# When the softmax sums are added: some adds moved behind the reciprocals, and one of GpSimd's adds moved to VectorE

## The chip, the cores and the metric

The kernel runs on one core of a Trainium2 chip. Its five compute engines run side by side, each through its own list of instructions, and meet by semaphores: TensorE (PE; PEld is its weight load), VectorE (DVE), ScalarE (ACT), GpSimd (POOL) and SyncE (SP), which here only starts DMA transfers. The metric is the device time of one execution in microseconds (us). Lower is better.

## The reference

Attention with normalised queries and keys for 8 batches, 12 heads, 448 tokens and a head size of 64; then a "mixture of depths", in which a gate picks 128 of the 448 tokens of each batch and only those go through two layers.

```python
def rmsnorm(x, g):
    rms = np.sqrt(np.mean(x * x, axis=-1, keepdims=True) + 1e-06)
    return x / rms * g
q_n, k_n = (rmsnorm(q, g_q), rmsnorm(k, g_k))
scores = scale * np.matmul(q_n, k_n.transpose(0, 1, 3, 2))
scores = scores - np.max(scores, axis=-1, keepdims=True)
attn = np.exp(scores)
attn = attn / (np.sum(attn, axis=-1, keepdims=True) + 1e-09)
x = np.matmul(attn, v)                      # then (B, S, heads * 64)
# ...
scores = np.einsum('bsd,d->bs', x, w_gate)
out = x.copy()
for b in range(B):
    top_idx = np.argpartition(-scores[b], capacity)[:capacity]
    xe = x[b, top_idx]
    h = np.maximum(xe @ w1, 0.0)
    ye = h @ w2
    g = 1.0 / (1.0 + np.exp(-scores[b, top_idx]))
    out[b, top_idx] = x[b, top_idx] + g[:, None] * ye
```

The change is about one line of this, `np.sum(attn, axis=-1)`: the denominators of the softmax.

## The kernel before

Four heads of one batch are a group n (24 groups, three to a batch). A group's keys come in seven pieces of 64, and one piece is a unit, `u = 7 * n + i`. For each unit TensorE computes scores (16 matmuls for two units), ScalarE their exponentials `p`, and TensorE multiplies `p` with the values into `av`, which is summed over the seven units. The denominators take another path. The `p` of a group are added up elementwise, mostly on VectorE; then TensorE sums over the keys (`den_ps`), ScalarE copies the sums out, TensorE turns them (`denT_ps`), VectorE takes reciprocals (`rden`), and VectorE multiplies the turned values (`x_ps`) with them. That gives `x`.

Which engine adds what. In the first six groups GpSimd adds units 0 and 1 into a spare tile (named `tok` in the trace), VectorE adds units 2 to 5 and then GpSimd's tile to them, and unit 6 goes to TensorE as it is:

```python
def add_probs(u):
    n, i = divmod(u, NI)
    if i == NI - 1 and sums_last(n):
        lasts.setdefault(n, []).append(probs.pop(u))
        return
    first = 2 if by_pool(n) else 0
    if first and i == 1:
        t = first_tokens[n % 2].rearrange("p h i d -> p h (i d)")
        nc.gpsimd.tensor_tensor(out=t, in0=probs.pop(u - 1), in1=probs.pop(u), op=OP.add)    # L332
        firsts[n] = t
    elif i > first:
        begins = i == first + 1
        if begins:
            sums[n] = p_pool.tile([128, 2, S], F32, name="sum", bufs=2)
        nc.vector.tensor_tensor(                                                             # L338
            out=sums[n], in0=probs.pop(u - 1) if begins else sums[n], in1=probs.pop(u), op=OP.add
        )
        if first and i == NI - 2:
            nc.vector.tensor_tensor(out=sums[n], in0=sums[n], in1=firsts.pop(n), op=OP.add)  # L342

def sums_last(n):
    return n < 2 * NG or n == n_groups - 1       # NG = 3

def by_pool(n):
    return n < 2 * NG
```

The sums over the keys, the reciprocals, and `x`. In the early steps `denT_ps` and the second `x_ps` of a group lie in the same bank of PSUM (`ps_moe`, one buffer), and `den_ps` and the first `x_ps` in another (`ps_aux`, one buffer), with exceptions by the flag `spare`:

```python
def sum_keys(n):
    ps = aux([128, 512], "den_ps")
    terms = [sums.pop(n)] + lasts.pop(n, [])
    # ... 8 matmuls per term                     (L372)
    nc.scalar.copy(out=den.rearrange("d j p -> d (j p)"), in_=ps[:, 0 : S // 2])
    dens[n] = den
    if n < n_groups - 1:
        q, place = now
        when = (q, place + 1) if place == 0 or long_next(q) else (q + 1, 0)
        tasks.insert(0, (when, lambda: invert_sums(n)))

def invert_sums(n):
    den = dens.pop(n)
    # ... two transposes into denT_ps            (L397)
    nc.vector.reciprocal(out=rden, in_=ps[:CP]...)                                           # L399

def to_tokens(n, c):
    # ... four transposes into x_ps              (L415)
    nc.vector.tensor_tensor(out=xs[b]..., in0=ps[:CP]..., in1=rdens[n]..., op=OP.mult)       # L417
```

The order of the work. A step q computes the scores of four units in two halves and lets the values of earlier units follow. `opening(q, place)` runs at most one or two due tasks: a group's tasks are `sum_keys` in the step in which its last unit is done, `invert_sums` and `to_tokens(n, 0)` at the start of the next, and then `to_tokens(n, 1)` with the gate. `run(slots)` issues the preparation of later groups: squares, `ss`, powers (`rinv`), scaled queries (`qT`) and loads. Instructions stay in the order in which they are issued, engine by engine:

```python
def before_layers(q):
    return done == 0 and ready.get(0, q + 1) > q       # the first batch's layers haven't begun

def run_values(upto, q):
    ended = False
    while waiting and waiting[0] <= upto:
        u = waiting[0]
        if ended and u % NI == 0:
            return
        values(waiting.pop(0))
        if u % NI == NI - 1:
            values_out(u // NI)
            finish(u // NI, q)
            ended = True
        add_probs(u)

while done < B or tasks:
    now[:] = q, 0
    k = PER * q                                        # PER = 4
    for half in range(HALVES):                         # HALVES = 2
        for u in (k + 2 * half, k + 2 * half + 1):
            if u < units:
                scores(u)
        run_values(k + 2 * half - 1, q)
    opening(q, 0)
    for half in range(HALVES):
        slots = (k + 2 * half, k + 2 * half + 1)
        if not short(q):
            run(slots)
        some = piece(q)                                # a piece of the two layers
        spare[0] = not some and half == 0
        if some or half == 0 or len(tasks) > 2:
            opening(q, half + 1)
        spare[0] = False
        run(slots)
    q += 1
```

Of the kernel before, what the change touches and what calls it, by code (L numbers as in the profile page):

```python
# [68 lines left out]
def fast(  # L69
# [30 lines left out]
    NG = H // GH  # L100
# [183 lines left out]
    def scores(u):  # L284
        n, i = divmod(u, NI)
        scs = [ps_sc.tile([128, 512], F32, tag="sc", name="sc") for _ in range(2)]


        for c in range(2):
            for hh in (1, 0):  # L290
                r = slice(D * hh, D * (hh + 1))
                nc.tensor.matmul(  # L292
                    out=scs[hh][D * c : D * (c + 1), 0:S],
                    lhsT=get("kT", n)[r, c, D * i : D * (i + 1)],
                    rhs=get("qT", n)[r, c, :],
                    start=True,
                    stop=True,
                )
        p = p_pool.tile([128, 2, S], F32, name="p")
        for hh in range(2):  # L300
            nc.scalar.activation(  # L301
                out=p[:, hh],
                in_=scs[hh][:, 0:S],
                func=AF.Exp,
                scale=rinvs[n, 1][:, hh, i : i + 1],
            )
        probs[u] = p

    def values(u):
        n, i = divmod(u, NI)  # L310
        if i == 0:
            avs[n] = [ps_av.tile([128, 512], F32, name="av") for _ in range(2)]
        for hh in (1, 0):
            for c in range(2):
                r = slice(D * c, D * (c + 1))
                nc.tensor.matmul(  # L316
                    out=avs[n][c][D * hh : D * (hh + 1), 0:S],
                    lhsT=get("v", n)[r, hh, i, :],
                    rhs=probs[u][r, hh],
                    start=(i == 0),  # L320
                    stop=(i == NI - 1),
# [22 lines that stand above are left out]
    def values_out(n):  # L344
        for c in (1, 0):
            t = norm_pool.tile([128, NJ, CP], F32, name="xT", bufs=4)
            nc.scalar.copy(out=t.rearrange("d j p -> d (j p)"), in_=avs[n][c][:, 0:S])
            xTs[n, c] = t
        avs.pop(n)

    dens, lasts, firsts = {}, {}, {}
# [3 lines left out]
    def sums_last(n):  # L355


        return n < 2 * NG or n == n_groups - 1

    def by_pool(n):  # L360

        return n < 2 * NG

    def sum_keys(n):

# [270 lines left out]
    HALVES = 2  # L636
# [12 lines left out]
    def opening(q, place):  # L649
        now[:] = q, place  # L650
        for _ in range(2):
            for i, (when, fn) in enumerate(tasks[:2]):
                if when <= (q, place):
                    tasks.pop(i)
                    waited = len(dens)
                    fn()
                    if place == 0 and len(dens) < waited:

                        break
                    return  # L660
                if i == 0 and dens:

                    return
# [27 lines left out]
    def finish(n, q):  # L691

        if n == n_groups - 1:
            for fn, args in ((sum_keys, (n,)), (invert_sums, (n,)), (to_tokens, (n, 0))):
                task((q, 1), fn, *args)
            task((q, 1), last_tokens, n)
            return
        task((q, 1), sum_keys, n)
        task((q + 1, 0), to_tokens, n, 0)
        task((q + 1, 1), last_tokens, n)  # L700
# [7 lines left out]
    def before_layers(q):  # L708
        return done == 0 and ready.get(0, q + 1) > q
# [33 lines left out]

        return -(-(units + 2 * PER - NG * NI * (B - 2 - b)) // PER)

    def run_values(upto, q):
        ended = False
        while waiting and waiting[0] <= upto:
            u = waiting[0]
# [5 lines that stand above are left out]
                values_out(u // NI)  # L755
                finish(u // NI, q)
                ended = True
            add_probs(u)

    for i in range(2):  # L760
        sum_squares(0, i, squares(0, i))
# [6 lines left out]
    def run(slots):  # L768
        for slot in sorted(x for x in todo if x < 0 or x in slots):
            for fn in todo.pop(slot):  # L770
                fn()

    def short(q):

        return pieces[0] == 1

    def piece(q):

        nonlocal moe, done
        if q in begin and pieces[0] > 2 and half == 1:  # L780
            return False
        pieces[0] += 1
        if next(moe, moe) is not moe:
            return True
        if ready.get(done, q + 1) > q:
            return False
        moe = mixture(done)
        done += 1
        pieces[0] = 1
        next(moe)  # L790
        return True
# [5 lines left out]
    moe, ready, done, q = iter(()), {}, 0, 0  # L797
    while done < B or tasks:
        now[:] = q, 0
        k = PER * q  # L800
        for half in range(HALVES):
            for u in (k + 2 * half, k + 2 * half + 1):
                if u < units:
                    scores(u)
            run_values(k + 2 * half - 1, q)
        opening(q, 0)
        for half in range(HALVES):
            slots = (k + 2 * half, k + 2 * half + 1)
            if not short(q):
                run(slots)  # L810
            some = piece(q)
# [6 lines that stand above are left out]
# [457 lines left out]
def _build(nc, ap, cap, out):  # L1275
    D = ap["g_q"].shape[0]
    with tile.TileContext(nc) as tc, ExitStack() as ctx:
        load_pool = ctx.enter_context(tc.tile_pool(name="load", bufs=1))
        with tc.tile_pool(name="bound", bufs=1) as pool:
            g = pool.tile([1, 2, D], F32, name="g")  # L1280
            nc.sync.dma_start(out=g, in_=ap["g_row"])
            loads = Loads(nc, load_pool, *(ap[n] for n in ("qT", "kT", "vp", "tok", "g2")))


            prod = pool.tile([1, D], F32, name="prod")
            nc.vector.tensor_mul(out=prod, in0=g[:, 0], in1=g[:, 1])
            nc.vector.tensor_mul(out=prod, in0=prod, in1=prod)
            top = pool.tile([1, 1], F32, name="top")
            nc.vector.tensor_reduce(out=top, in_=prod, axis=AX.X, op=OP.max)
            small = pool.tile([1, 1], I32, name="small")  # L1290
            nc.vector.tensor_scalar(
                out=small,
                in0=top,
                scalar1=MAX_SCORE * MAX_SCORE / D,
                scalar2=None,
                op0=OP.is_le,
            )
            is_small = nc.values_load(small[0:1, 0:1], min_val=0, max_val=1,
                skip_runtime_bounds_check_because="a comparison gives 0 or 1")
        with tc.If(is_small > 0) as cmp, tc.manual_schedule():  # L1300
            fast(
                tc, loads, *(ap[n] for n in _INS[5:]), cap, out,
            )
        with cmp.Else():
            general(tc, *(ap[n] for n in _INS), cap, out)
# [45 lines left out]
```

## Time and profile before

| | |
|---|---|
| time, median of 3 runs | 525.54 us (523.82 to 526.93) |
| span of the profiled run | 523.3 us |
| busy of TensorE, VectorE, ScalarE, GpSimd | 504.8, 339.9, 277.6, 195.7 us |
| mean granted clock of TensorE | 0.995 |
| GpSimd's adds (L332) | 6, mean 2240 ns |
| VectorE's adds (L338, the most common form) | 101, mean 1090 ns |
| VectorE's adds of GpSimd's tile (L342) | 6, mean 1408 ns |

The profile is one execution. A line of a timeline gives the start and the length in us, the engine, the line of the kernel, the operation, what it writes and reads, and in brackets how long its engine had stood idle and what ended that. A line of the waits gives who waited for whom, the total in us, how often, and the longest. A line of the window table gives the stretch, its length, and for PE, PEld, DVE, ACT and POOL the busy us and instructions; then the clock granted to TensorE as a share of full speed, the share of the DMA engines and GB/s. The line numbers are those of the whole kernel; the comments above repeat the ones that matter.

### The profile page before, as it was taken

Reading aid. Unit: us, or ns where it says so; the run is one execution under the profiler, and the core shown is the slowest. Engines: PE = TensorE matmul, PEld = TensorE weight load, DVE = VectorE, ACT = ScalarE, POOL = GpSimd, SP = SyncE. Lnnn points to the kernel's source line nnn. Section 1 sums busy time; section 2 is a strip of 40 time slices with the busy share of each in tenths; the row PEclk is TensorE's granted clock in tenths of the full one; section 3 lists DMA queues with packets and bytes.
Section 4 is the critical chain, followed back from the end, with each engine's and each line's share of the span. In section 5 each row is a group of like instructions: output and inputs, shape, how many; then the busy total and the mean of one; then the engine's idle time right before and its main releaser. Section 6 shows DMA issues by size and latency. Waiting matters only on the chain.

```text
span 523.3 us, 10988 instructions
## 1 busy us (share of the span) xinstructions
PE 504.8 (96%) x4421; PEld 296.2 (57%) x4421; DVE 339.9 (65%) x636; ACT 277.6 (53%) x507; POOL 195.7 (37%) x110
## 2 busy tenths in 40 slices
PE   5999898999999999999999999999999999999995
PEld 4544343465744476446654467544764447659694
DVE  4578798879755995649666787467946487335100
ACT  4887875857535845556544675645463474411100
POOL 4897768433522363133612434305621103002102
PEclk9999998999999999999999999999999999999999
DMA  8977879979843846629627677423942231004100
GB/s 297 371 240 265 290 245 361 329 239 316 279 138 88 258 155 210 191 86 278 218 61 188 179 232 234 127 87 115 295 141 72 71 137 37 26 0 151 55 24 36
DMA packets 43406, 93.21 MB, mean 178 GB/s; under 512 B 11060, under 2 KB 23349, under 8 KB 43347
## 3 DMA queue, kind: packets, MB, share of 16 engines
q1 hardware_dynamic: 39938, 86.11, 52.5%
q0 software_dynamic: 3264, 6.31, 3.4%
q8 instruction: 37, 0.61, 0.5%
q14 instruction: 23, 0.18, 0.1%
q10 hardware_dynamic: 144, 0.00, 0.0%
HBM read 74.93 MB, written 25.35 MB: 192 GB/s over the span
## 4 chain that ended last, share of the span: by engine, by line
PE 90%; DVE 6%; DMA 2%; issue 1%; POOL 0%; ACT 0%; SPq 0%; DVEq 0%; POOLq 0%; ACTq 0%
PE sc L292 25%; PE av L316 23%; PE moe_ps L582 13%; PE moe_ps L602 11%; PE sc L582 4%; PE x_ps L415 4%; PE sc L602 4%; PE den_ps L372 3%; PE denT_ps L397 1%; DVE sum L338 1%; DMA out_dram<-xe,row 1%; DVE sum L342 1%; DVE ss L219 1%; DVE x L417 1%; PE sc L262 1%
## 5 line engine op out<-in xcount | busy, mean ns | idle before, releaser
L301 ACT ACTIVATE p<-sc,rinv 128x448 f32<-128x448 f32 x336 | 186.5, 643 | 104.1 <-PE sc L292 90.6
L220 POOL TENSOR_TENSOR rinv<-ss,neg_half 128x14 f32<-128x14 f32 (+1 forms) x49 | 129.0, 2639 | 191.3 <-DVE ss L219 188.4
L292 PE MATMUL sc<-qT,kT 64*64 64x448 f32 x1344 | 156.6, 548 | 1.2 <-DVE qT L271 0.8
L316 PE MATMUL av<-p,v 64*64 64x448 f32 x1344 | 149.2, 537 | 0.0
L338 DVE TENSOR_TENSOR sum<-sum,p 128x896 f32<-128x896 f32 x101 | 110.1, 1090 | 7.1 <-ACT p L301 0.7
L316 PEld LDWEIGHTS av<-p,v 64*64 64x64 f32 x1344 | 60.3, 133 | 67.6 <-issue 57.4
L292 PEld LDWEIGHTS sc<-qT,kT 64*64 64x64 f32 x1344 | 55.0, 133 | 71.3 <-issue 45.4
L582 PE MATMUL moe_ps<-xeT,w 128*128 128x128 f32 x576 | 69.3, 277 | 0.0
L582 PEld LDWEIGHTS moe_ps<-xeT,w 128*128 128x128 f32 x576 | 66.2, 192 | 5.3 <-issue 5.3
L219 DVE TENSOR_REDUCE ss<-sq 128x14 f32<-128x910 f32 (+1 forms) x49 | 52.3, 1074 | 22.9 <-ACT sq L210 22.9
L602 PE MATMUL moe_ps<-w,hT 128*128 128x384 f32 x176 | 61.3, 491 | 0.4 <-DVE xe L611 0.3
L417 DVE TENSOR_TENSOR x<-x_ps,rden 112x512 f32<-112x512 f32 x48 | 32.8, 689 | 37.4 <-PE x_ps L415 36.6
L513 POOL DMA_INDIRECT selected<-x,rank x32 | 34.5, 1077 | 50.2 <-DVE x L505 42.2
L210 ACT ACTIVATE sq<-tok 128x896 f32<-128x896 f32 (+1 forms) x49 | 46.5, 953 | 5.9 <-DMA tok<-in_tok_dram 5.8
L602 PEld LDWEIGHTS moe_ps<-w,hT 128*128 128x128 f32 x176 | 31.7, 190 | 22.5 <-issue 2.5
L441 DVE SCALAR_TENSOR_TENSOR prod<-x,wg 112x256 f32<-112x256 f32 x96 | 40.7, 424 | 3.0
L621 POOL DMA_INDIRECT out_dram<-xe,row x10 | 12.2, 1222 | 77.7 <-DVE rden L399 47.3
L415 PE MATMUL x_ps<-ident,xT 128*112 128x128 f32 x192 | 29.5, 279 | 2.2 <-DVE rden L399 2.2
L338 DVE TENSOR_TENSOR sum<-p 128x896 f32<-128x896 f32 x24 | 27.8, 1158 | 4.6 <-ACT p L301 4.6
L251 DVE SCALAR_TENSOR_TENSOR qT<-qT,gg,bc 128x896 f32<-128x896 f32 x22 | 27.4, 1245 | 4.5 <-DMA bc<-rows 4.5
L611 DVE SCALAR_TENSOR_TENSOR xe<-sc,xe 128x384 f32<-128x384 f32 (+1 forms) x6 | 3.3, 551 | 40.6 <-PE sc L602 40.6
L415 PEld LDWEIGHTS x_ps<-ident,xT 128*112 128x112 f32 x192 | 21.8, 135 | 11.5 <-issue 7.7
(69 smaller groups left out, 309.8 us busy)
## 6 DMA issues: line engine op xcount, KB each, us to landing
tok<-in_tok_dram SPq DMA_DIRECT2D x48, 448.0 KB, 6.3
qT<-in_qT_dram SPq DMA_DIRECT2D x24, 448.0 KB, 4.9
kT<-in_kT_dram SPq DMA_DIRECT2D x24, 448.0 KB, 8.1
v<-in_vp_dram SPq DMA_DIRECT2D x24, 448.0 KB, 8.7
out_dram<-x SPq DMA_DIRECT2D x8, 1344.0 KB, 8.4
bc<-rows SPq DMA_DIRECT2D x44, 224.0 KB, 7.0
xe<-selected SPq DMA_DIRECT2D x8, 385.0 KB, 3.8
w<-in_moe_w_dram SPq DMA_DIRECT2D x6, 512.0 KB, 8.2
```

Source lines behind the costliest of these rows:

```text
L210: nc.scalar.activation(out=sq[:, h, :, 0:D], in_=t[:, h], func=AF.Square, scale=scale)
L219: nc.vector.tensor_reduce(out=ss[:, h], in_=sq[:, h], axis=AX.X, op=OP.add)
L220: nc.gpsimd.tensor_tensor(out=rinv[:, h].rearrange(flat), in0=ss[:, h].rearrange(flat), in1=neg_half.to_broadcast([128, (h.stop - h.start) ...
L292: nc.tensor.matmul(out=scs[hh][D * c : D * (c + 1), 0:S], lhsT=get("kT", n)[r, c, D * i : D * (i + 1)], rhs=get("qT", n)[r, c, :], start=True,
L301: nc.scalar.activation(out=p[:, hh], in_=scs[hh][:, 0:S], func=AF.Exp, scale=rinvs[n, 1][:, hh, i : i + 1],)
L316: nc.tensor.matmul(out=avs[n][c][D * hh : D * (hh + 1), 0:S], lhsT=get("v", n)[r, hh, i, :], rhs=probs[u][r, hh], start=(i == 0), stop=(i ...
L338: nc.vector.tensor_tensor(out=sums[n], in0=probs.pop(u - 1) if begins else sums[n], in1=probs.pop(u), op=OP.add)
L415: nc.tensor.transpose(out=ps[:CP, j, :], in_=t[:, j, :], identity=ident)
L417: nc.vector.tensor_tensor(out=xs[b][:, :, col : col + 128].rearrange("p j (h d) -> p j h d", d=D), in0=ps[:CP].rearrange("p j (h d) -> p j ...
L441: nc.vector.scalar_tensor_tensor(out=prod, in0=xs[b][:, j, cols], scalar=1.0, in1=wg[:, cols], op0=OP.mult, op1=OP.mult, accum_out=gates[b ...
L582: nc.tensor.matmul(out=ps[:, 128 * i : 128 * i + n], lhsT=w1[:, dc, 128 * (f0 + i) : 128 * (f0 + i + 1)], rhs=xeT[:, dc, :n], start=(dc == 0),
L602: nc.tensor.matmul(out=ps[:n, :width], lhsT=hT[:, fc, :n], rhs=w2[:, fc, cols], start=(fc == 0), stop=(fc == NFC - 1),)
```

## The change

It does two things. In a step in which a denominator waits to be inverted, and before the layers of the first batch have begun, the adds that belong to the second half are not issued at once but after `opening(q, 0)`, which holds the reciprocal and the first multiplication into `x`. So VectorE finds the reciprocal ahead of these adds. And GpSimd adds in five groups instead of six: in group 5 all of units 0 to 5 are added by VectorE. The purpose is that TensorE need not wait for a reciprocal that stands behind adds, and that VectorE and GpSimd get less in each other's way. Nothing of the computation is left out; the order in which group 5 is added up differs.

```diff
     def by_pool(n):
 
-        return n < 2 * NG
+        return n < 2 * NG - 1
@@
-    def run_values(upto, q):
+    adds = []
+
+    def add_all():
+        for u in adds:
+            add_probs(u)
+        adds.clear()
+
+    def run_values(upto, q, late):
         ended = False
         while waiting and waiting[0] <= upto:
             u = waiting[0]
@@
                 finish(u // NI, q)
                 ended = True
-            add_probs(u)
+            adds.append(u)
+            if not late:
+                add_all()
@@
             for u in (k + 2 * half, k + 2 * half + 1):
                 if u < units:
                     scores(u)
-            run_values(k + 2 * half - 1, q)
+
+            late = half == HALVES - 1 and len(dens) > 0 and before_layers(q)
+            run_values(k + 2 * half - 1, q, late)
         opening(q, 0)
+        add_all()
         for half in range(HALVES):
             slots = (k + 2 * half, k + 2 * half + 1)
             if not short(q):
```

## The prediction

> **What bounds the kernel now.** I read the page's busy table first, then the window table, then the waits of the first 110 us, and last the timelines of TensorE and VectorE there.
>
> ```profile
> PE 504.8 (96%) x4421; PEld 296.2 (57%) x4421; DVE 339.9 (65%) x636; ACT 277.6 (53%) x507; POOL 195.7 (37%) x110
> ```
>
> TensorE is the bound overall; the window table says where it still idles.
>
> ```profile
> 42.00:58.00 16.00, 14.40 (x162) 6.10 (x154) 13.57 (x28) 11.58 (x22) 10.58 (x4) 1.00 0.82 276
> ...
> 70.00:86.00 16.00, 12.79 (x130) 5.98 (x126) 15.27 (x29) 10.44 (x20) 9.43 (x6) 0.96 0.99 343
> ...
> 110.00:470.00 360.00, 359.25 (x3086) 208.03 (x3085) 245.71 (x460) 192.97 (x357) 112.97 (x59) 1.00 0.52 157
> ```
>
> The second number is busy TensorE. From 110 to 470 us it idles 0.75 us: what the change shifts before 110 us arrives at the end one for one. From 70 to 86 us VectorE is busy 15.27 of 16 us and TensorE idles 3.2. The waits of 0 to 110 us name the two partners (total us, times, longest):
>
> ```profile
> PEld den_ps L372 <- DVE sum L342: 3.6, 2, 2.4
> ...
> PEld x_ps L415 <- DVE rden L399: 2.9, 4, 2.4
> ...
> PE den_ps L372 <- DVE sum L342: 2.6, 2, 1.6
> ...
> PE x_ps L415 <- DVE rden L399: 2.2, 1, 2.2
> ```
>
> TensorE waits for the reciprocal (which the change puts ahead of adds), but also for the sums themselves (which the change puts off). TensorE's timeline places them:
>
> ```profile
> 41.83 0.58 PE L372 MATMUL den_ps<-sum,pick_pair 128*32 128x224 f32 x8 [0.22 <-DVE x L417]
> ...
> 57.35 0.59 PE L372 MATMUL den_ps<-sum,pick_pair 128*32 128x224 f32 x8 [1.60 <-DVE sum L342]
> ...
> 74.66 0.58 PE L372 MATMUL den_ps<-sum,pick_pair 128*32 128x224 f32 x8 [1.03 <-DVE sum L342]
> ...
> 84.78 1.10 PE L415 MATMUL x_ps<-ident,xT 128*112 128x128 f32 x4 [2.19 <-DVE rden L399]
> ```
>
> These are den_ps of groups 1, 2 and 3, and x_ps of group 3. VectorE's timeline shows who stood ahead of each reciprocal:
>
> ```profile
> 39.05 1.29 DVE L342 TENSOR_TENSOR sum<-sum,tok 128x896 f32<-128x896 f32 x1
> 40.64 0.26 DVE L399 RECIPROCAL rden<-denT_ps 112x16 f32<-112x16 f32 x1 [0.30 <-PE denT_ps L397]
> ...
> 49.36 0.26 DVE L399 RECIPROCAL rden<-denT_ps 112x16 f32<-112x16 f32 x1 [1.17 <-PE denT_ps L397]
> ...
> 65.64 0.26 DVE L399 RECIPROCAL rden<-denT_ps 112x16 f32<-112x16 f32 x1 [1.90 <-PE denT_ps L397]
> ...
> 81.07 2.29 DVE L338 TENSOR_TENSOR sum<-sum,p 128x896 f32<-128x896 f32 x2
> 83.46 1.09 DVE L342 TENSOR_TENSOR sum<-sum,tok 128x896 f32<-128x896 f32 x1
> 84.47 0.25 DVE L399 RECIPROCAL rden<-denT_ps 112x16 f32<-112x16 f32 x1
> ...
> 90.24 3.30 DVE L251 SCALAR_TENSOR_TENSOR qT<-qT,gg,bc 128x896 f32<-128x896 f32 x1 [1.24 <-DMA bc<-rows]
> ```
>
> Three reciprocals (groups 0, 1, 2) come to an *idle* VectorE, which waits for TensorE's denT_ps. Only the fourth (group 3) is held up by adds.
>
> [...] the reciprocal at 84.47 runs behind the adds although denT_ps ended at 82.15. [...] qT at 90.24 took 3.30 us beside a GpSimd add of 90.51 to 92.58, against 1.15 elsewhere. [...] from 81.3 to 84.7 TensorE was busy 1.29 of 3.4 us, and from 84.7 to 88.1 the clock was 0.50; 54.0 to 57.4 with 1.80 busy was followed by 1.00.
>
> **The change part by part.** Write k = 4q for step q. The flag needs a waiting denominator at the second half; walking tasks and units gives steps 3, 4, 6 and 8. Which adds move follows from u = 7n + i:
>
> *q = 3, units 12 and 13 (i = 5, 6 of group 1).* Moved: one sum (1.1 us) and the L342 add (1.1). The reciprocal at 40.64 waits for TensorE anyway: nothing is won. But den_ps of group 1, in the same step, reads this sum. Before, it started at 41.83; now VectorE ends x at 41.77, then 1.1 + 1.1, so den_ps starts at about 44.05. TensorE, free from 41.6, stands still 2.45 us: **+2.2**.
>
> *q = 4, units 16 and 17.* Moved: one sum (1.1) from the 1.17 us hole ahead of 49.36 to behind x. From 49.80 to 57.31 the chain of waits runs on VectorE without a hole and ends in den_ps of group 2. So **+1.1**; that stall grows from 1.60 to 2.7.
>
> *q = 6, units 24 and 25.* Moved: two sums (2.2) from the 1.90 us hole ahead of 65.64 to behind x at 66.08. From there VectorE is again full until L342 ends at 74.60, with the GpSimd add in it (starts 70.75, after its own pow at 68.19, which waits for the ss behind x). All move together: **+2.2** on den_ps of group 3, whose stall grows from 1.03 to about 3. The wait of ScalarE for GpSimd at 68.26 (2.15 us) goes, worth some 0.3 on TensorE.
>
> *q = 8, units 32 and 33.* Moved: two sums and L342 (3 × 1.15 = 3.4 us) from before to behind the reciprocal of group 3. It then waits only for denT_ps, and x_ps starts about 2.2 earlier, and the half clock after it is less likely. This is the purpose: **−2.2**, up to −1.7 more for the clock. What follows keeps only part: the next reciprocal (101.08) is 16.6 us after this one, 14.5 of it VectorE work. The 3.4 us now fall into that stretch.
>
> *Five groups instead of six.* Group 5 had a GpSimd add (2.07) and four VectorE adds; now five VectorE adds: +1.1 on VectorE. In exchange qT loses its block (3.30 − 1.15 = 2.15), and waits of 1.24 + 0.25 + 0.66 fill up. Stretch after: 16.6 − 2.15 − 2.15 + 1.1 + 3.4 = 16.8, about what it was. So the −2.2 of q = 8 stays, but no clock gain on top: TensorE waits for VectorE there (den_ps of group 5 needs x).
>
> Sum: 2.2 + 1.1 + 2.2 − 0.3 − 2.2 = **+3.0 us**.
>
> *Clock.* Three stalls of 2.5, 2.7 and about 3 us replace one of 2.19 and two short ones. [...] I take 2.1 dips, less 0.5; a dip costs at most 1.7 us, on average perhaps 0.8 since part of it falls on waiting: **+1.3**.
>
> From 525.5: 525.5 + 3.0 + 1.3 = **529.8 us**, 0.8% slower.
>
> **Rivals.** *It does what it is for:* the 84.78 stall and its half clock go (−4 us) and the new waits find slack that I overlook, so 521.5 to 523. For it: the largest single stall is this one, and the half clock after it is in the trace. Against it: den_ps of groups 1, 2 and 3 read exactly the delayed sums, and two already wait. *Nothing moves:* VectorE's work is nearly the same (+1.1 − 2.15), its holes are merely elsewhere, and TensorE absorbs 2 us in the shadow of VectorE from 86 to 103 us: 524 to 527. For it: 96% TensorE. Against it: nothing after 110 us takes up a delay. *More throttling:* each new stall costs its full 1.7 us, and DMA (share 1.0 from 86 to 110 us) shifts: 533 to 535.
>
> **Range and chances.** The spread before is 523.82 to 526.93. I give my own sum two thirds, the first rival a fifth, the rest to the others: 524.0 to 533.5. Two per cent is 10.5 us; the whole idle time of TensorE before 110 us beyond the start is about 5 us, so faster by 2% is out, and slower by 2% would take three times my sum: 0.01, 0.96, 0.03.
>
> **What would show it.** Right: in TensorE's timeline den_ps of group 1 (near 44) with an idle of about 2.4 us on sum L342, den_ps of group 2 near 61 with 2.7, of group 3 near 80 with 3, and the wait of x_ps for rden of 2.19 gone; the total of den_ps waits for DVE sum rising from 2.6 to 7 or 8 us; clock at half after at least one of them; qT at 1.15 us everywhere; five GpSimd adds on L332. From 110 us on, everything shifted by one constant. Wrong: den_ps of group 1 starting within 0.5 us of x_ps (then the sum was not moved or not needed there), or reciprocals 0 to 2 that also start earlier, or a shift that shrinks after 110 us.

## The result, and the profile after

The changed kernel takes 532.29 us (median of 6 runs, 530.59 to 533.74); the kernel before took 524.94 us beside it (6 runs, 523.41 to 526.93). The ratio is 1.0136, with a 95% interval of 1.0105 to 1.0168: 7.3 us slower, within 2%. The prediction said 529.8 us, within 524.0 to 533.5. The profiled run of after has a span of 530.9 us, against 523.3.

TensorE's timeline of after, with the same matmuls as were shown of before (start and length in us, and in brackets the idle time ahead and what ended it), and the scores that follow the first of them:

```profile
44.27 0.69 PE L372 MATMUL den_ps<-sum,pick_pair 128*32 128x224 f32 x8 [2.49 <-DVE sum L342]
...
45.63 2.90 PE L292 MATMUL sc<-qT,kT 64*64 64x448 f32 x16
...
62.42 0.58 PE L372 MATMUL den_ps<-sum,pick_pair 128*32 128x224 f32 x8 [2.60 <-DVE sum L342]
...
82.09 0.95 PE L372 MATMUL den_ps<-sum,pick_pair 128*32 128x224 f32 x8 [3.72 <-DVE sum L342]
...
92.09 0.65 PE L415 MATMUL x_ps<-ident,xT 128*112 128x128 f32 x4 [0.43 <-issue]
```

The three den_ps stalls were 0.22, 1.60 and 1.03 us and are now 2.49, 2.60 and 3.72. The 2.19 us wait of x_ps for the reciprocal is gone. VectorE's timeline of after shows how the first stall comes about: the reciprocal of group 0 finds VectorE idle for 3.79 us, and the two adds that den_ps of group 1 needs stand behind it.

```profile
40.81 0.26 DVE L399 RECIPROCAL rden<-denT_ps 112x16 f32<-112x16 f32 x1 [3.79 <-PE denT_ps L397]
41.25 0.69 DVE L417 TENSOR_TENSOR x<-x_ps,rden 112x512 f32<-112x512 f32 x1 [0.18 <-PE x_ps L415]
41.86 1.08 DVE L338 TENSOR_TENSOR sum<-sum,p 128x896 f32<-128x896 f32 x1
43.03 1.09 DVE L342 TENSOR_TENSOR sum<-sum,tok 128x896 f32<-128x896 f32 x1
```

The waits of the first 120 us of after, who for whom (total us, times, longest):

```profile
DVE rden L399 <- PE denT_ps L397: 13.3, 4, 4.9
...
PE den_ps L372 <- DVE sum L342: 8.8, 3, 3.7
```

VectorE waits for TensorE ahead of the reciprocals (4.1 us in the first 110 us before, 13.3 in these 120 us now), then TensorE waits for VectorE behind them (2.6 before, 8.8 now).

The sixteen score matmuls at 45.63 take 2.90 us; before they took 1.73. The window table of after says why: the third number from the end is the clock granted to TensorE, as a share of full speed.

```profile
42.00:44.20 2.20, 0.00 (x0) 0.00 (x0) 2.11 (x3) 0.35 (x1) 0.00 (x0) 1.00 0.86 225
44.20:47.10 2.90, 2.83 (x24) 1.17 (x28) 2.88 (x5) 0.34 (x1) 1.82 (x1) 0.57 0.99 342
```

The clock falls to half (0.50) right behind the stall, when there is work again: from 44.6 to 48.0 us. The same happens from 82.1 to 85.5 us (0.51), behind the stall of group 3. A stretch of this kind is called half clock below.

Where the time came in, from the two timelines (differences of starts, less the 0.17 us by which after's den_ps of group 0 begins later):

| up to | after minus before, us | step |
|---|---|---|
| den_ps of group 1 | 2.27 | stall of q = 3: +2.27 |
| denT_ps of group 1 | 3.90 | half clock: +1.63 |
| den_ps of group 2 | 4.90 | stall of q = 4, 5: +1.00 |
| denT_ps of group 2 | 4.90 | full clock |
| den_ps of group 3 | 7.26 | stall of q = 6, 7: +2.36 |
| denT_ps of group 3 | 8.90 | half clock: +1.64 |
| second x_ps of group 3 | 7.14 | reciprocal of q = 8: −1.76 |
| den_ps of group 4 | 6.87 | before's own half clock gone, most of it lost again: −0.27 |
| den_ps of group 5 | 7.11 | wait for x: +0.24 |
| end | 7.4 | |

### The profile page after: what moved, and what is told of

It is laid out like the page before. It is cut to its first block, busy times and chain, and to the rows that moved or that the text cites. A ratio compares the mean times of both kernels' runs of the same rounds, so it can differ in the third digit from the quotient of the medians.

```text
span 530.9 us, 10987 instructions
## 1 busy us (share of the span) xinstructions
PE 508.3 (96%) x4421; PEld 296.7 (56%) x4421; DVE 338.0 (64%) x637; ACT 277.7 (52%) x507; POOL 190.6 (36%) x109
## 4 chain that ended last, share of the span: by engine, by line
PE 82%; DVE 7%; issue 1%; DMA 0%; ACT 0%; POOL 0%; DVEq 0%; POOLq 0%; ACTq 0%
PE sc L292 21%; PE av L316 20%; PE moe_ps L582 12%; PE moe_ps L602 11%; PE sc L602 4%; PE sc L582 4%; PE x_ps L415 4%; PE den_ps L372 3%; DVE sum L338 2%; PE denT_ps L397 1%; DVE ss L219 1%; DVE x L417 1%; DVE prod L441 1%; DVE sum L342 1%; PE row_ps L470 1%
## 5 line engine op out<-in xcount | busy, mean ns | idle before, releaser
L292 PE MATMUL sc<-qT,kT 64*64 64x448 f32 x1344 | 158.8, 552 | 1.4 <-DVE qT L271 0.8
L338 DVE TENSOR_TENSOR sum<-sum,p 128x896 f32<-128x896 f32 x103 | 113.7, 1104 | 7.0 <-ACT p L301 0.7
L399 DVE RECIPROCAL rden<-denT_ps 112x16 f32<-112x16 f32 x24 | 6.1, 255 | 38.0 <-PE denT_ps L397 33.8
L338 DVE TENSOR_TENSOR sum<-p 128x896 f32<-128x896 f32 x24 | 25.9, 1078 | 4.6 <-ACT p L301 4.6
L380 ACT COPY den<-den_ps 128x224 f32<-128x224 f32 x24 | 8.4, 348 | 38.5 <-PE den_ps L372 38.4
```

What stands on the lines that cost most here:

```text
L292: nc.tensor.matmul(out=scs[hh][D * c : D * (c + 1), 0:S], lhsT=get("kT", n)[r, c, D * i : D * (i + 1)], rhs=get("qT", n)[r, c, :], start=True,
L338: nc.vector.tensor_tensor(out=sums[n], in0=probs.pop(u - 1) if begins else sums[n], in1=probs.pop(u), op=OP.add)
```

## The experiments

The theories: **A**, the cost comes from the sums put off in steps 3, 4 and 6, on which den_ps waits, with half clock behind the longer stalls, and step 8 alone is a gain. **B**, it comes from group 5, which VectorE now adds alone. **C**, a late add costs wherever it is, and what is won at the reciprocal is lost on VectorE soon after. D to G came up on the way and are told in the expectations. Each edit is against the changed kernel. Nothing of the computation is left out in any of them. Runs 1 to 4, then 9 to 12, then 5 to 8 were made beside the kernel before, which took 524.77, 525.23 and 524.55 us there (27, 31 and 71 executions). The ratios are to that.

**1. No late adds, five groups.**

```diff
-            late = half == HALVES - 1 and len(dens) > 0 and before_layers(q)
+            late = half == HALVES - 1 and len(dens) > 0 and before_layers(q) and False
```

> Five groups, no late adds. Theory A: qT of group 6 takes 1.15 us and not 3.3, one VectorE add of 1.1 us is new, the stretch from the reciprocal of group 3 to that of group 4 gets some 1 us shorter, and the time is 523.5 to 525.5 us. Rival B: near the changed kernel, 530 us or more.

Measured: 524.69 us (14 runs), ratio 1.0002 (0.9989 to 1.0015). The fifth group makes no difference by itself, and rival B falls. In VectorE's timeline qT of group 6 takes 1.15 us instead of 3.30, but then VectorE waits 1.60 and 0.66 us for squares from ScalarE where it waited 0.25 and 0.66: the time set free is not used.

**2. All late adds, six groups.**

```diff
-        return n < 2 * NG - 1
+        return n < 2 * NG
```

> Late adds in all four steps, six groups on GpSimd as before. Theory A: within 1.5 us of the changed kernel, 531 to 534 us, with the same three den_ps stalls. Rival B: near before, 525 us.

Measured: 530.99 us (4 runs), ratio 1.0108 (1.0078 to 1.0138), with stalls of 2.49, 2.60 and 3.73 us. The late adds alone make the loss.

**3. Late in step 8 alone.**

```diff
-            late = half == HALVES - 1 and len(dens) > 0 and before_layers(q)
+            late = half == HALVES - 1 and len(dens) > 0 and before_layers(q) and q == 8
```

> Five groups on GpSimd, adds late in step 8 alone. Theory A (the cost comes from the sums put off in steps 3, 4 and 6, on which den_ps waits; step 8 alone is a gain): the three den_ps stalls are those of before (0.2, 1.6, 1.0 us), the 2.19 us wait of x_ps for the reciprocal of group 3 is gone, and the time is 522 to 523.5 us, 1.5 to 3 us below before. Rival B (the cost comes from group 5, which VectorE now adds alone): still slower than before, 527 us or more. Rival C (a late add costs wherever it is, what is won at the reciprocal is lost again within two steps): 524 to 526 us.

Measured: 524.25 us (14 runs, 522.02 to 529.03), ratio 1.0010 (0.9981 to 1.0039). This is what C expected, and A's gain of 1.5 to 3 us did not come. But it is not VectorE that takes the gain. In the trace den_ps of group 4 starts at 89.54 instead of 93.26 us, so 3.7 us are won. They are lost at one place, where TensorE's timeline of this kernel reads:

```profile
100.34 0.55 PE L554 MATMUL moe_ps<-ident,xe 128*128 128x128 f32 x3 [2.86 <-DMA xe<-selected]
```

These are the first matmuls on the 128 selected rows of batch 0. In the kernel before, TensorE's timeline has them at about the same time:

```profile
101.20 0.55 PE L554 MATMUL moe_ps<-ident,xe 128*128 128x128 f32 x3
```

There TensorE's weight load had stood 0.25 us for them: the rows land at about the same time in both (the waits end at about 100.3 and 101.2 us). SyncE issues their load at 94.89 us here and at 93.24 before, and the DMA engines are fully busy around it (their share from 90 to 100 us is 0.99 here and 1.04 before). A new theory, **E**: the arrival of the selected rows sets the time of step 10 (with late adds in step 8 alone).

**4. Late in steps 3, 4 and 6, not in 8** (`and q != 8`).

> Five groups, adds late in steps 3, 4 and 6 but not in 8. Theory A: the three long den_ps stalls (2.5, 2.6, 3.7 us) stay and the 2.2 us wait of x_ps for the reciprocal of group 3 comes back: 533.5 to 535 us, 1.5 to 3 us above the changed kernel. Rival B: the same 532 us as the changed kernel. Rival C: 530 to 532 us, a little better than the changed kernel, since one late step less.

Measured: 531.96 us (4 runs), ratio 1.0117 (1.0082 to 1.0152). The three stalls are there (2.49, 2.60 and 3.73 us), and with late adds in these steps alone the whole loss is there. A's addition of 1.5 to 3 us for the missing late adds of step 8 did not come; the time is the one that B and C gave. TensorE's timeline shows that x_ps of group 3 doesn't wait at all in this execution, though step 8 has no late adds:

```profile
83.52 0.97 PE L372 MATMUL den_ps<-sum,pick_pair 128*32 128x224 f32 x8 [3.73 <-DVE sum L342]
...
93.86 1.16 PE L415 MATMUL x_ps<-ident,xT 128*112 128x128 f32 x8
```

From den_ps to x_ps TensorE needs 10.3 us here instead of 7.3 before, since the clock is at half from 82.9 to 89.75 us, twice as long as in after. VectorE is through with its adds by then. So in this execution the gain that step 8 is meant for was not there to be had once the earlier steps had slowed TensorE down. It is the longest of the four, so in the others something of the wait may be left.

**5 to 7. Late in one of the steps 3, 4 and 6** (`and q == 3`, and so on).

> Five groups, adds late in step 3 alone. Theory A (each step costs what its sum is late, plus half clock behind a stall of 2 us or more): den_ps of group 1 waits 2.5 us, the other two 1.6 and 1.0 as before, and the time is 526.5 to 529 us. Rival G (the stalls of steps 3, 4 and 6 hang together, VectorE catches up in the next hole): under 526 us.

Measured: 526.69 us (20 runs), ratio 1.0046 (1.0032 to 1.0061).

> Five groups, adds late in step 4 alone. Theory A: den_ps of group 2 waits 2.6 us instead of 1.6, den_ps of groups 1 and 3 as before, and the time is 525.5 to 527.5 us. Rival G: under 525.5 us.

Measured: 525.32 us (20 runs), ratio 1.0005 (0.9987 to 1.0023): the time is rival G's, though den_ps of group 2 waits 2.60 us, as A said.

> Five groups, adds late in step 6 alone. Theory A: den_ps of group 3 waits 3.3 to 3.7 us instead of 1.0, with half clock after it; x_ps of group 3 then waits less for its reciprocal (under 1.5 us instead of 2.2), because a TensorE at half clock gets there later; the time is 526.5 to 528.5 us, and steps 3, 4 and 6 alone add up to the 7 us of all three. Rival G: under 526 us.

Measured: 526.40 us (20 runs), ratio 1.0028 (1.0015 to 1.0040). This lies between A's range and G's. The stalls of the late steps are as A has them; here den_ps of group 1 with step 3 late, and den_ps of group 3 with the scores that follow it with step 6 late:

```profile
44.01 0.58 PE L372 MATMUL den_ps<-sum,pick_pair 128*32 128x224 f32 x8 [2.49 <-DVE sum L342]
```

```profile
77.68 0.98 PE L372 MATMUL den_ps<-sum,pick_pair 128*32 128x224 f32 x8 [3.73 <-DVE sum L342]
...
79.33 3.27 PE L292 MATMUL sc<-qT,kT 64*64 64x448 f32 x16
```

and x_ps of group 3 waits 2.19 us with step 3 or 4 late and not at all with step 6 late. But the sizes fall short. The three ratios add up to 0.8%, 4.1 us, and not to the 6 to 7 us of the three together, so A's sum fails. Nor do the runs show A's mark of 2 us for half clock, which was the author's estimate: in the traces of steps 3 and 4 alone the clock stayed at 1.00 behind the long stall, with the same lengths of 2.49 and 2.60 us that were followed by half clock elsewhere (group 2's 2.60 in runs 2 and 4, not in after). And step 6 alone hides part of its loss in the reciprocal's wait of 2.19 us. Step 4's effect is within its interval. That the rest of the gap is half clock that comes together more often when stalls follow one another is argued, not shown.

The half clock behind the stall of group 3 is also longer here than in after. With step 6 late it lasts from 76.5 to 83.3 us, in runs 2 and 4 equally 6.8 us, and begins 0.6 to 1.2 us before the work. From den_ps to denT_ps of group 3 these three traces need 9.8 to 10.1 us, against 8.70 in after and 7.06 before.

**8. Late in step 8 alone, six groups** (run 3 with `return n < 2 * NG`).

> Six groups on GpSimd as before, adds late in step 8 alone. Theory E (the selected rows set the time of step 10, what VectorE does before it is hidden): as with five groups, 523.5 to 525.5 us, though qT of group 6 is blocked again by GpSimd's add (over 2 us). If the fifth group were needed for the gain of step 8, den_ps of group 5 waits for VectorE and the time is 526 us or more.

Measured: 524.75 us (20 runs, 520.75 to 528.48), ratio 0.9999 (0.9973 to 1.0025), with 2.52 us of waiting for the selected rows. E holds. The block of qT did not come back, though; its line in the trace:

```profile
L251 DVE SCALAR_TENSOR_TENSOR qT<-qT,gg,bc x1: 1148/1148/1148, 90.3 to 90.3; 128x896 f32<-128x896 f32 x1
```

1.15 us, with GpSimd's sixth add still in the kernel. Here it is GpSimd's add, from 90.63 us, that takes longer: 2.81 us instead of 2.07. In both kernels qT starts first (before at 90.24 us, ahead of an add from 90.51). So the 3.30 us of before are not a property of the six groups; what decides which of the two takes longer, no run shows.

**9. Keeping TensorE at work in the stalls.** All late adds, and idle transposes into the bank that den_ps then overwrites:

```diff
         terms = [sums.pop(n)] + lasts.pop(n, [])
+        for _ in range({1: 18, 2: 20, 3: 30}.get(n, 0)):
+            nc.tensor.transpose(out=ps[:, 0:128], in_=ident, identity=ident)
```

> The changed kernel with 18, 20 and 30 idle transposes (into the bank that den_ps then overwrites) ahead of den_ps of groups 1, 2 and 3, so that TensorE works through most of the three stalls. Theory A (the half clock behind the stalls is on the path and costs 1.6 us each time): the clock stays at 1.00 between 42 and 100 us, den_ps of the three groups comes after the same sums, and the time falls by 2.5 to 3.5 us against the changed kernel, to 528.5 to 530 us. Rival D (the slow stretches fall into time in which TensorE would wait for VectorE anyway): 531.5 to 533 us.

Measured: 527.98 us (6 runs, 527.57 to 528.48), ratio 1.0049 (1.0033 to 1.0066), against 1.0136 for the changed kernel: 68 matmuls more, and some 4.5 us less. TensorE's timeline of this kernel (its lines after L368 lie two further down):

```profile
41.44 2.18 PE L369 MATMUL den_ps<-ident 128*128 128x128 f32 x18 [0.22 <-DVE x L419]
43.63 0.58 PE L374 MATMUL den_ps<-sum,pick_pair 128*32 128x224 f32 x8
44.03 0.56 PE L374 MATMUL den_ps<-p,pick_pair 128*32 128x224 f32 x8
44.52 1.73 PE L292 MATMUL sc<-qT,kT 64*64 64x448 f32 x16
```

The sums come as late as in after, but the scores run in 1.73 us and not in 2.90. The clock is 1.00 all the way:

```profile
42.00:58.00 16.00, 16.00 (x166) 7.75 (x165) 13.29 (x29) 9.65 (x18) 8.37 (x4) 1.00 0.83 282
58.00:70.00 12.00, 11.73 (x124) 6.11 (x126) 6.64 (x8) 8.45 (x15) 10.25 (x4) 1.00 0.71 245
70.00:86.00 16.00, 15.53 (x166) 8.40 (x162) 15.44 (x33) 11.26 (x22) 6.04 (x3) 1.00 1.01 338
```

So rival D falls: what goes with the half clock is more than half of the 7.3 us, and A's own estimate for it (2.5 to 3.5 us) was still too low. The single executions agree: the shortest of after and of runs 4 and 2 (530.59, 528.61 and 529.17 us) have a mean granted clock of 0.993 to 0.995, the longest (533.74, 532.82 and 533.81 us) one of 0.985 to 0.989.

Runs 10 and 11 have the edit of run 3 besides the one shown; run 12 has the edits of run 1 and of run 11. In 11 and 12 `store_x` takes the tile as an argument; the lines for that are left out.

**10. Step 8 alone, the first layers one step later.**

```diff
-        ready[b] = max((s + 8) // PER + 1, first_ff(b) - 1 if b else 0) if b < B - 1 else 0
+        ready[b] = max((s + 8) // PER + (2 if b == 0 else 1), first_ff(b) - 1 if b else 0) if b < B - 1 else 0
```

> Five groups, late adds in step 8 alone, and the layers of the first batch begin one step (4 units) later. Theory E (what step 8 wins is lost to the wait of TensorE for the selected rows of the first batch, 2.9 us with late adds in step 8 alone, because these rows land at the same time as before): that wait is gone and the time is 520 to 522.5 us, unless the shifted layers cost at the end. Rival C (what is won at the reciprocal is lost on VectorE within two steps): a new wait on VectorE near den_ps of group 5, 523.5 to 525.5 us.

Measured: 523.65 us (8 runs), ratio 0.9965 (0.9949 to 0.9982). TensorE no longer waits for the selected rows, which E expected, but the time is 1.15 us above E's range and within C's: the second x_ps of group 4 now waits 1.36 us for its reciprocal. So VectorE does take back a part, as C said.

**11. Step 8 alone, the store of batch 0 later.**

```diff
-        at(s + 4 if s >= 0 else s, store_x, b)
+        at(s + (16 if b == 0 else 4) if s >= 0 else s, store_x, b, xs[b])
```

> Five groups, late adds in step 8 alone, and the 1.3 MB store of the first batch's x issued 12 slots (three steps) later, behind the load of the selected rows; nothing else moves. Theory E: with 1.3 MB less ahead of them the selected rows land 2 to 4 us earlier, the 2.9 us wait of TensorE for them shrinks under 1 us, and the time is 519.5 to 522 us. Rival C: 523.5 to 525.5 us.

Measured: 523.04 us (6 runs, 522.59 to 523.84), ratio 0.9956 (0.9939 to 0.9973): faster than before and after. From TensorE's timeline of this kernel:

```profile
97.54 0.49 PE L554 MATMUL moe_ps<-ident,xe 128*128 128x128 f32 x3
...
99.86 0.59 PE L372 MATMUL den_ps<-sum,pick_pair 128*32 128x224 f32 x8 [1.07 <-DVE x L417]
```

The wait for the selected rows is gone, and the first matmuls on them start 3.7 us earlier than before. Then the wait that the prediction named takes over: den_ps of group 5 waits 1.07 us for x, because VectorE has work from one reciprocal to the next (82.24 and 98.76 us). The time lies between E's range (519.5 to 522 us) and C's. The start of group 5's den_ps is 2.6 us earlier than before, and the median 2.2.

**12. The later store alone, no late adds.**

> Five groups, no late adds, the same later store. Theory E: TensorE did not wait for the selected rows without late adds in step 8 (0.2 us at most), so the later store alone is worth nothing: 523.5 to 525.5 us. If it is itself a gain (rival F: fewer transfers in the way of qT and tok), 520 to 522.5 us.

Measured: 524.24 us (22 runs), ratio 0.9983 (0.9971 to 0.9996): the time is in E's range, but 0.9 us better than before and clear of it, so of the 0.44% of run 11 about 0.17% is not due to the late adds; F expected far more. x_ps of group 3 waits for its reciprocal as ever:

```profile
84.70 0.65 PE L415 MATMUL x_ps<-ident,xT 128*112 128x128 f32 x4 [2.19 <-DVE rden L399]
```

The four matmuls behind the same wait of 2.19 us took 1.10 us before, at half clock, and 0.65 here, at full clock. That run 12 gains because half clock is rarer there would fit (the mean clock is 0.997 to 0.999 in the 14 executions of up to 524.5 us, and 0.993 to 0.995 in the other 8), but isn't shown.

Left open: the times of runs 3 and 8 spread over 7.0 and 7.7 us, against 1.25 in run 11, and only one execution of each has a trace. The longer ones have a lower clock: those of 527 us or more have a mean clock of 0.990 to 0.993, those under 523 us one of 0.996 to 0.999. That the selected rows land later in them would fit, but isn't shown.

## Why the prediction was right, and where its sizes were off

**The steps 3, 4 and 6.** Predicted +2.2, +1.1 and +2.2 (less 0.3), measured +2.27, +1.00 and +2.36 in the trace (the last with the 0.3 taken off). The reading that found them was: see where VectorE stood idle ahead of a reciprocal. Three of the four had nothing to win, and the moved adds went from a hole to a place where den_ps waited for them.

**Step 8, −2.2.** The wait went, as said, and x_ps came 1.76 us nearer. That VectorE takes back the clock gain was right in kind: den_ps of group 5 waits for x in after, run 9 and run 11 (0.39, 1.07 and 1.07 us). But the prediction overlooked a second taker, the arrival of the selected rows. In before TensorE stands only 0.25 us for them; with late adds in step 8 alone the wait grows to 2.86 us and eats most of the gain (run 3). It plays no part in after, where TensorE is 7 us later than before. There the late adds of step 8 bring nothing measurable, 532.29 us with and 531.96 without (run 4), and in run 4's trace the slowed TensorE doesn't wait for the reciprocal anyway.

**Five groups.** The prediction had the stretch from the reciprocal of group 3 to that of group 4 about even, 16.8 us; in after it is 16.84 (91.78 to 108.62 us), and the fifth group alone leaves the time even (run 1). The 2.15 us for qT were real (1.15 us in after and in run 1), but qT took 1.15 us with six groups too (run 8).

**The sum without the clock, +3.0.** Run 9, which has all stalls and no half clock, is 2.75 us above before by the medians and 2.9 us by the spans.

**The clock, +1.3.** This is the term that was mis-sized. The prediction counted 2.1 stretches, an estimate of the author's that no trace shows. It is about what after's trace has (two between 42 and 110 us, where the mean clock is 0.95). But it put a stretch at 0.8 us, "since part of it falls on waiting". In after nothing of it falls on waiting: the half clock begins within 0.4 us of the work and lasts about 3.4 us, and the two cost 1.63 and 1.64 us. Nor is 1.7 us, half of the 3.4 us at half clock in before, the most that one costs, as the prediction had it: in runs 2, 4 and 7 the stretch behind the long stall lasts 6.8 us and costs 2.7 to 3.0. And the 0.5 stretch taken off for before was no credit, as the prediction itself had said under "no clock gain on top": from the second x_ps of group 3 to den_ps of group 5 after needs 17.63 us at full clock and before 17.66 with the half clock, since with late adds in step 8 den_ps of group 5 waits for VectorE's x. Without them the half clock did count: in run 12, at full clock, the same way takes 16.16 us and that wait is not there. Run 9 puts the whole term at some 4.5 us; the two stretches account for 3.3 of it, and the rest is spread over the steps behind them. With that in place of 1.3 the prediction would have read 533.0; measured is 532.3. A slip in its last part: the 10.5 us of two per cent are 2.4 times the 4.3 us of its whole sum, not three times.

Two things weren't foreseen and are small. The second x_ps of group 3, at 92.09 us, starts 0.05 us after the end of the reciprocal, which itself starts 0.56 us after denT_ps has ended. And the way from the scores at 92.67 us to den_ps of group 4 takes 7.63 us, for which run 3 needs 6.63: ScalarE's exponentials of the first scores begin 2.11 us after these, against 1.10 in run 3, and the next scores (95.46 us) start as the first exponential ends. Why the reciprocal and the exponentials start late stays unexplained.

## What to carry to other kernels

Before an instruction is moved ahead of others on an engine that runs them in the order of issue, as VectorE did here (in before the reciprocal at 84.47 us ran behind the adds, though denT_ps had ended at 82.15), look at whether that engine is idle when the favoured instruction comes, and at who reads the ones that are put off: a rule that is meant for one place may cost at three others, so apply it by place. Where an engine comes earlier because a stall is gone, look for the next arrival that had been just in time, here the transfer of the selected rows (2.86 us of waiting in run 3), and move that too. And expect that a stall of TensorE can cost more than its length: here those of 2.19 to 2.60 us were in part followed by half clock (worth 1.63 us behind the 2.49 in after), and those of 3.7 us in all four traces that have them, worth 1.6 to 3.0 us.

## What the runs showed that was not expected

Work for nothing made the changed kernel faster: 68 transposes whose output is overwritten took some 4.5 us off. Equal stalls were not followed by equal clocks: 2.49 us by half clock in after and by full clock in run 5, 2.19 us by half clock before and by full clock in run 12; the 2.86 us of waiting for the selected rows in run 3 were followed by full clock too. Only the long stall of 3.7 us was followed by half clock in every trace that has it (after and runs 2, 4 and 7). The half clock behind it lasted 3.4 us in after and twice that, 6.8, in runs 2, 4 and 7. What sets the length, and why equal stalls fare differently, no run here shows.
